# FFN1's half-word weight copies on GpSimd, and a new load and rank order, in a fused attention and two-FFN kernel

## The chip, the cores and the metric

One core of a Trainium2 chip runs the whole program. The metric is the device time of one execution in microseconds (us). The core has five engines with their own instruction streams, which run in order and meet through semaphores: TensorE (PE, products), VectorE (DVE), ScalarE (ACT), GpSimd (POOL) and SyncE (SP, which here issues nearly all DMAs).

## The reference, cut to what matters

Windowed attention (4 batches, 8 heads, 576 positions, window 64), then two feed-forward layers over 2304 tokens of width 512.

```python
def _attn_ref(q, k, v):                       # (4, 8, 576, 64) each
    scores = scale * np.matmul(q, k.transpose(0, 1, 3, 2))
    mask = (rel >= 0) & (rel < 64)
    scores = np.where(mask, scores, -1000000000.0)
    ...                                       # softmax
    return np.matmul(attn, v)

def _moe_ref(x, w_in, w_out):                 # FFN1: 512 -> 2048 -> 512
    h = np.maximum(x @ w_in, 0.0)
    return h * h @ w_out

def _moe2_ref(x, w_in, w_out, g_ln):          # FFN2: 512 -> 1024 -> 512
    h = x @ w_in
    ...                                       # softmax over h, h * softmax, layer norm with g_ln
    return ln @ w_out
```

The weights of both layers are 64-bit floats in memory. The kernel makes each into a 32-bit number by bit operations, and then into a pair (high part, rest), so that one product of 32-bit accuracy is three products on TensorE.

## The kernel before, in words

Sequence blocks of 64 positions are taken two at a time, a *unit*. Attention for the first four units (eight blocks) and FFN1 over their 512 tokens come first; units 4 and later are computed among FFN1's products and put aside in DRAM. The rest of FFN1 runs in two passes of 768 and 1024 tokens by a scheme with seven instead of eight block products, and then FFN2.

FFN1's 32 weight tiles are 16 of `w_in` (kind "a") and 16 of `w_out` (kind "b"), 128 x 512 each. A tile goes through `assembled` and `weights`:
- `load`: SyncE loads the raw 64-bit tile, 512 KB, into one of four `wraw` buffers;
- `top` (the *half-word copy*, a CAST at L260): every fourth 16-bit word of the raw tile is copied into the upper halves of a 32-bit tile `top`, of which there are two that take turns;
- `rest` (L265): VectorE shifts the raw tile's other words and ORs `top` in (SCALAR_TENSOR_TENSOR); this frees the raw buffer and the `top` tile;
- `first` (L283): ScalarE writes the high part, `wa` or `wb`; `second` (L286): VectorE writes the rest.

The products with `wa` are `ps_h` (L690), those with `wb` are `ps_y` (L706). Before them ScalarE and VectorE make the pair of x (`high`, `rest`, L530 and L533), and between them relu, square and the pair `g` (L636, L639). A unit of attention is scores (`ps_s`, L435), maximum, exponentials (L450), normalisation (`e<-e,sums`, L460), transposes (`ps_p`, L476 and L478), a copy, and values (`ps_v`, L516 to L521). For later units the normalisation is GpSimd's.

The order of all instructions comes from a planner, `Plan`: each step is added with its engine, an estimated length, a rank, what it follows and which buffers it takes and gives; `run` picks the step that can start first, the lower rank first, and `emit` writes the steps in that order. A step with `port=True` is not planned beside another such step. A table, `SHIFT`, adds a number to the ranks of single steps. Where TensorE would be idle in the plan, dummy products on a tile of ones (`ps_warm`, L1781) are put: 51 *fillers* in all, in the first part and late. `TOPS` is 16, the number of tiles of each kind, so VectorE makes all 32 half-word copies. The variable `by_dve` says so, and the copy is planned with the port.

Of the kernel before, what the change touches and what calls it, by code (L numbers as in the profile page):

```python
# [26 lines left out]
class Plan:  # L27
# [7 lines left out]

    HOP = {"DVE": 0.16, "ACT": 0.14, "POOL": 0.35, "PE": 0.12, "SP": 0.1}
    GAP = {"DVE": 0.1, "ACT": 0.1}
    SHIFT = {0: 13.59, 43: 8.08, 162: -11.77, 188: 6.06, 192: -3.28, 195: 10.82, 198: 10.82, 214: 13.42, 260: -3.43, 263: -3.43, 331: -39.05,
# [6 lines left out]

    def __init__(self, slots):
        self.tasks, self.slots = [], {k: [0.0] * n for k, n in slots.items()}
# [1 line left out]
    def add(self, eng, us, rank, fn, after=(), take=(), give=(), port=False, late=0.0, at=0.0):  # L49
        t = dict(eng=eng, us=us, rank=rank + self.SHIFT.get(len(self.tasks), 0.0), fn=fn, after=[a for a in after if a], take=take, give=give, port=port, late=late, at=at,  # L50
                 start=None, n=len(self.tasks))
        self.tasks.append(t)
        return t
# [51 lines left out]
def kernel(  # L105
# [48 lines left out]
    V, S, G, T = nc.vector, nc.scalar, nc.gpsimd, nc.tensor  # L154
# [47 lines left out]
    with ExitStack() as c1:  # L202
# [16 lines left out]
        add = plan.add  # L219
# [5 lines left out]
        def assembled(kind, i, rank, after=()):  # L225
            early = kind == "a" and i < EARLY
            ringed = kind in "ab"
            by_dve = ringed and i < TOPS
            o = {}

            def load():
                o["raw"] = raw_p.tile([P, 1024], I32, tag="wraw", name="wraw", bufs=RAWS)
                nc.sync.dma_start(out=o["raw"].bitcast(U16)[:, : 4 * DM - 1], in_=SRC[kind][i][:, 1:])

            def home():
                if kind == "a":
                    if i // 2 not in w1:
                        w1[i // 2] = w1_p.tile([P, 2, 512], F32, tag="w1", name="w1")
                    o["m"] = w1[i // 2][:, i % 2]
                elif kind == "2o":  # L240
                    w2o[i] = w1_p.tile([P, 2, 512], F32R, tag="w1", name="w2o")
                    o["m"] = at_p.tile([P, 512], F32, tag="qk"[i % 2], name="w2m", bufs=1)
                else:
                    o["m"] = raw_p.tile([P, 512], F32, tag="wm", name="wm", bufs=WMB)
                if not ringed:
                    G.memset(o["m"], 0.0)

            def top():
                if ringed:
                    home()  # L250
                    if not tops:
                        tops.append(x_p.tile([P, 2, 512], F32, tag="xc", name="top", bufs=1))
                        G.memset(tops[0], 0.0)
                    o["turn"] = turns.pop(0)
                    o["t"] = tops[0][:, o["turn"]]
                else:
                    o["t"] = o["m"]
                to, word = o["t"].bitcast(F16)[:, 1::2], o["raw"].bitcast(BF16)[:, 2::4]
                if by_dve:
                    V.tensor_copy(to, word)  # L260
                else:
                    S.activation(out=to, in_=word, func=AF.Copy)

            def rest():
                V.scalar_tensor_tensor(out=o["m"].bitcast(I32), in0=o["raw"][:, ::2], scalar=13, in1=o["t"].bitcast(I32),  # L265
                                       op0=ALU.logical_shift_right, op1=ALU.bitwise_or)
                if ringed:
                    turns.append(o["turn"])

            a = add("SP", 1.7, rank - (LEAD if early else 9), load, after, take=["raw"], late=LATE, at=0.7)  # L270
            own = {"a": [], "2o": ["qk"[i % 2] + "2"]}.get(kind, ["wm"])
            z = [] if ringed else [add("POOL", 0.6, rank - 3, home, [a], take=own, port=True)]
            b = add(*(("DVE", 0.36) if by_dve else ("ACT", 0.77)), rank, top, [a, *z], take=["top", *own] if ringed else [], port=by_dve)
            return o, add("DVE", 0.62, rank, rest, [b], port=True, give=["raw", "top"] if ringed else ["raw"])

        def weights(kind, i, rank, after=()):
            pool, store = {"a": (wa_p, wa), "b": (wb_p, wb)}[kind]
            o, c = assembled(kind, i, rank, after)
            made[kind, i] = c

            def first():
                o["d"] = pool.tile([P, 2, 512], F32R, tag="wb" if kind == "b" else "wa", name=f"w{kind}")
                S.activation(out=o["d"][:, 0, :], in_=o["m"], func=AF.Copy)  # L283

            def second():
                V.tensor_tensor(out=o["d"][:, 1, :], in0=o["m"], in1=o["d"][:, 0, :].bitcast(F32), op=ALU.subtract)  # L286
                store[i] = o["d"]

            b = add("ACT", 0.54, rank, first, [c], take=["wa"] * (kind == "a"))
            ready[kind, i] = add("DVE", 0.61, rank, second, [b], port=True, give=["wm"] * (kind == "b"))  # L290
# [3 lines left out]
        def kept_w2(kind, i, rank, after):  # L294
            o, c = assembled(kind, i, rank, after)

            def store():
                nc.sync.dma_start(out=w2_dram[i], in_=o["m"])

            made[kind, i] = add("SP", 0.8, rank, store, [c], late=2.2, give=["wm"])  # L300

        def last_w2(kind, i, rank, after):
            o, c = assembled(kind, i, rank, [*after, *read_w[i]])

            def high():
                S.activation(out=w2o[i][:, 0], in_=o["m"], func=AF.Copy, scale=gcol[:, i : i + 1])

            def low():
                V.scalar_tensor_tensor(out=w2o[i][:, 1], in0=o["m"], scalar=gcol[:, i : i + 1], in1=w2o[i][:, 0].bitcast(F32), op0=ALU.mult,
                                       op1=ALU.subtract)  # L310

            c = add("ACT", 0.54, rank, high, [c])
            ready[kind, i] = add("DVE", 0.61, rank, low, [c], port=True, give=["qk"[i % 2] + "2"])
# [1017 lines left out]
        LATE, LATE_X, LATE_P, TOPS = 2.8, 4.43, 4.63, KF  # L1331
# [4 lines left out]
        LOADS = (10.92, 14.03, 17.81, 25.72, 19.77, 31.14)  # L1336
        CHUNKS = (15.8, 24.78, 29.24)
        V0, LATER, OUT = 5.26, 51.93, 2.41
        LEAD = 22.21
        SOON, EARLIER, LATE_POOL = 11.15, 0, False  # L1340
        WOS, WOL, WSL, SQ, P2AT, P4AT, SOON2, SOON3, LEAD2 = 3, 8, 8, 5, 13, 17, 14, 6, 3
        PUT, PUT0, PUT1, AGO, LATEB, WOP = 16, 10, 3, 0, 145, 12
# [492 lines left out]
```

## Time and profile before

| | us |
|---|---|
| time, median of 3 runs | 628.54 (628.41, 628.54, 631.99) |
| profiled execution, its time | 629.19 |
| its span, first to last instruction | 627.4 |
| TensorE busy | 619.7 (99%) |
| weight loads of TensorE busy | 523.8 (83%) |
| VectorE busy | 485.1 (77%) |
| ScalarE busy | 433.4 (69%) |
| GpSimd busy | 44.1 (7%) |

How to read it: matmuls are pipelined and their ends are modelled, so TensorE's busy time is not work at its peak; the fillers count as busy too. A wait shows as idle time in front of an instruction, with what ended it. The granted clock was full in every slice of the page. Spans on GpSimd are rough.

### The profile page before, as it was taken

Reading aid. Unit: us, or ns where it says so; the run is one execution under the profiler, and the core shown is the slowest. Engines: PE = TensorE matmul, PEld = TensorE weight load, DVE = VectorE, ACT = ScalarE, POOL = GpSimd, SP = SyncE. Lnnn points to the kernel's source line nnn. Section 1 sums busy time; section 2 is a strip of 40 time slices with the busy share of each in tenths; the row PEclk is TensorE's granted clock in tenths of the full one; section 3 lists DMA queues with packets and bytes.
Section 4 is the critical chain, followed back from the end, with each engine's and each line's share of the span. In section 5 each row is a group of like instructions: output and inputs, shape, how many; then the busy total and the mean of one; then the engine's idle time right before and its main releaser. Section 6 shows DMA issues by size and latency. Waiting matters only on the chain.

```text
span 627.4 us, 11566 instructions
## 1 busy us (share of the span) xinstructions
PE 619.7 (99%) x4009; PEld 523.8 (83%) x4009; DVE 485.1 (77%) x1129; ACT 433.4 (69%) x985; POOL 44.1 (7%) x80
## 2 busy tenths in 40 slices
PE   8999999999999999999999999999999999999997
PEld 4798888889999989998888887878788888888886
DVE  5999898297876762397988999998998986687440
ACT  5788777577877675467677676873787875776551
POOL 1000000001212110000000000000001110110010
PEclk9999999999999999999999999999999999999999
DMA  8888988446899999877688556985255565532351
GB/s 278 275 293 297 309 291 282 128 176 230 278 296 329 291 327 286 296 260 217 211 285 266 196 162 230 311 253 170 100 169 177 176 218 169 200 135 88 115 184 50
DMA packets 85450, 141.26 MB, mean 225 GB/s; under 512 B 7824, under 2 KB 49552, under 8 KB 85392
## 3 DMA queue, kind: packets, MB, share of 16 engines
q1 hardware_dynamic: 84704, 140.14, 67.7%
q8 instruction: 31, 0.51, 0.3%
q10 hardware_dynamic: 688, 0.39, 0.2%
q14 instruction: 27, 0.22, 0.1%
HBM read 90.69 MB, written 49.81 MB: 224 GB/s over the span
## 4 chain that ended last, share of the span: by engine, by line
PE 90%; DMA 4%; DVE 3%; ACT 1%; issue 1%; SPq 1%; ACTq 0%; DVEq 0%
PE ps_h L935 21%; PE ps_o L1706 16%; PE ps_h L1545 14%; PE ps_y L1255 11%; PE ps_y L1069 8%; PE ps_y L706 7%; PE ps_h L690 6%; PE ps_s L435 3%; PE ps_v L518 2%; PE ps_v L521 1%; PE ps_warm L1781 1%; PE ps_p L478 1%; DMA kt<-in_k 1%; DMA qk<-in_k 1%; DMA r<-r_dram 1%
## 5 line engine op out<-in xcount | busy, mean ns | idle before, releaser
L1706 PE MATMUL ps_o<-w2o,lnT 128*128 128x512 f32 x432 | 99.2, 389 | 0.0
L1706 PEld LDWEIGHTS ps_o<-w2o,lnT 128*128 128x128 f32 x432 | 81.1, 188 | 16.9
L1255 PE MATMUL ps_y<-g,wb 128*128 128x384 f32 x384 | 71.9, 335 | 0.0
L1255 PEld LDWEIGHTS ps_y<-g,wb 128*128 128x128 f32 x384 | 66.8, 188 | 0.7 <-issue 0.3
L1545 PE MATMUL ps_h<-w2i,xx 128*128 128x512 f32 x243 | 62.6, 390 | 0.0
L1069 PE MATMUL ps_y<-g,wb 128*128 128x512 f32 x234 | 58.2, 390 | 0.1
L935 PE MATMUL ps_h<-xa,wo 128*128 128x512 f32 (+1 forms) x192 | 53.5, 370 | 0.1
L1545 PEld LDWEIGHTS ps_h<-w2i,xx 128*128 128x128 f32 x243 | 45.6, 188 | 9.6
L1069 PEld LDWEIGHTS ps_y<-g,wb 128*128 128x128 f32 x234 | 43.7, 188 | 10.1 <-DVE wb L1043 0.5
L935 PE MATMUL ps_h<-xb,wo 128*128 128x384 f32 (+1 forms) x192 | 51.0, 356 | 0.0
L706 PE MATMUL ps_y<-g,wb 128*128 128x512 f32 (+1 forms) x240 | 47.8, 352 | 0.0
L690 PE MATMUL ps_h<-x,wa 128*128 128x512 f32 (+1 forms) x240 | 47.4, 351 | 0.0
L935 PE MATMUL ps_h<-xo,wo 128*128 128x512 f32 (+1 forms) x128 | 47.2, 369 | 0.0
L450 ACT ACTIVATE e<-e,nmax 128x128 f32<-128x128 f32 x112 | 43.4, 390 | 2.6 <-DVE nmax L439 2.5
L690 PEld LDWEIGHTS ps_h<-x,wa 128*128 128x128 f32 x240 | 38.3, 189 | 6.6 <-issue 0.5
L706 PEld LDWEIGHTS ps_y<-g,wb 128*128 128x128 f32 x240 | 38.5, 189 | 6.0 <-issue 0.2
L935 PEld LDWEIGHTS ps_h<-xa,wo 128*128 128x128 f32 x192 | 35.2, 188 | 5.8 <-ACT u L959 0.8
L1695 ACT ACTIVATE lnT<-l 128x512 fp32r<-128x512 f32 x36 | 22.2, 627 | 24.3 <-PE ps_o L1706 22.0
L639 DVE TENSOR_TENSOR g<-r,g 128x384 fp32r<-128x384 f32 (+2 forms) x36 | 20.2, 566 | 22.6 <-ACT g L636 22.5
L935 PEld LDWEIGHTS ps_h<-xb,wo 128*128 128x128 f32 x192 | 34.4, 188 | 3.4 <-issue 0.3
L1545 PE MATMUL ps_h<-w2x,xx 128*128 128x512 f32 x135 | 36.8, 391 | 0.0
L1699 DVE TENSOR_TENSOR lnT<-l,lnT 128x512 fp32r<-128x512 f32 x36 | 24.1, 681 | 11.8 <-ACT lnT L1695 11.3
(182 smaller groups left out, 1257.9 us busy)
## 6 DMA issues: line engine op xcount, KB each, us to landing
wraw<-in_w_in SPq DMA_DIRECT2D x24, 511.8 KB, 5.6
wraw<-in_w_out SPq DMA_DIRECT2D x24, 511.8 KB, 5.4
vt<-in_v SPq DMA_DIRECT2D x32, 256.0 KB, 4.1
wo_dram<-wo SPq DMA_DIRECT2D x16, 512.0 KB, 5.1
wo<-wo_dram SPq DMA_DIRECT2D x16, 512.0 KB, 4.8
t_dram<-h SPq DMA_DIRECT2D x16, 512.0 KB, 3.0
l<-t_dram SPq DMA_DIRECT2D x64, 128.0 KB, 2.8
kt<-in_k SPq DMA_DIRECT2D x16, 384.0 KB, 5.5
```

Of the source, the lines that this page charges most:

```text
L435: T.matmul(to, qt[rows, i, hp, :], kt[rows, keys, hp, :], start=not begins, stop=not begins or hp == hps[-1])
L450: S.activation(out=o["er"][:, a, w], in_=s, func=AF.Exp, scale=SCALE if begins else -1.0, bias=o["nmax"][:, a, w : w + 1], accum_out=o["su ...
L639: V.tensor_tensor(out=o["g"][:, 1, :N], in0=o["r"], in1=o["g"][:, 0, :N].bitcast(F32), op=ALU.subtract)
L690: T.matmul(ps[:, :N], wa[kk][:, wi, c * P : c * P + P], xs[t][:, xi, c, n0:n1], start=n == 0, stop=n == 3 * DC - 1)
L706: T.matmul(acc[t, 0][d][:, n0:n1], wb[kk][:, wi, d * P : d * P + P], o["g"][:, xi, :N], start=kk == 0 and n == 0 and n0 == 0, stop=last an ...
L935: T.matmul(to[:, :N], w["t"][:, wi, off + c * P : off + c * P + P], (lo if xi else hi)()[:, c], start=begins and m == 0, stop=m == 5, skip ...
L1069: T.matmul(acc[name][d][:, :N], wb[kk][:, wi, col + d * P : col + d * P + P], q["g"][:, xi, :N], start=j == 0 and n == 0 and name not in ( ...
L1255: T.matmul(acc[t, half][d][:, :N], wb[kk][:, wi, d * P : d * P + P], q["g"][:, xi, :N], start=pos == 0 and n == 0, stop=pos == KF - 1 and ...
L1545: T.matmul(o[bank], o["xx", k][:, xi, at : at + P], w2i[w, r][wi][0](), start=begins and m == 0, stop=m == 5, skip_group_check=True)
L1695: S.activation(out=parts2(o["l", hf][:, 0]), in_=turned2(hf), func=AF.Copy)
L1699: V.tensor_tensor(out=parts2(l[:, 1]), in0=turned2(hf), in1=parts2(l[:, 0].bitcast(F32)), op=ALU.subtract)
L1706: T.matmul(o["o"], o["l", hf][:, xi, kk % 4, :], w2o[kk][:, wi, :], start=kk == 0 and n == 0, stop=kk == KF2 - 1 and n == 2)
```

## The change

Three things. Half-word copies of FFN1's weight tiles with an index of 2 or more (`POOLS = 2`; 14 of each kind, 28 of 32) are made by GpSimd (`G.tensor_copy`); the four with index 0 and 1 stay on VectorE. `SHIFT` holds other numbers, so the order on all engines is another. In SyncE's order the first unit's v goes behind the first q and k loads, and the second unit's v goes up in front of the weights.

```diff
-    SHIFT = {0: 13.59, 43: 8.08, 162: -11.77, 188: 6.06, 192: -3.28, 195: 10.82, 198: 10.82, 214: 13.42, 260: -3.43, 263: -3.43, 331: -39.05,
...
+    SHIFT = {0: -81.61, 6: 14.17, 10: -101.81, 19: -5.92, 20: -101.77, 37: 8.49, 55: -15.05, 160: -97.51, 161: -96.51, 162: -103.77, 177: 0.69,
...
-            by_dve = ringed and i < TOPS
+            by_dve, by_pool = ringed and i < TOPS, ringed and i >= POOLS
...
-                if by_dve:
+                if by_pool:
+                    G.tensor_copy(to, word)
+                elif by_dve:
                     V.tensor_copy(to, word)
...
-            b = add(*(("DVE", 0.36) if by_dve else ("ACT", 0.77)), rank, top, [a, *z], take=["top", *own] if ringed else [], port=by_dve)
+            b = add(*(("POOL", 0.6) if by_pool else ("DVE", 0.36) if by_dve else ("ACT", 0.77)), rank, top, [a, *z], take=["top", *own] if ringed else [], port=by_dve)
...
-        LEAD = 22.21
+        LEAD, POOLS = 22.21, 2
```

SyncE's first loads before (`vt` is v, `qt` and `kt` are q and k of a unit, `qk` those of the second unit, `wraw` a raw weight tile):

```order
L400 DMA vt_193<-in_v 64x512 x2
L383 DMA qt_198<-in_q 128x2x128 x2
L383 DMA qk_219<-in_q 128x2x256
L384 DMA qk_220<-in_k 128x2x256
L233 DMA wraw_237<-in_w_in 128x2047
L233 DMA wraw_255<-in_w_out 128x2047
L233 DMA wraw_294<-in_w_in 128x2047
L389 DMA qt_330<-in_q 128x512
L390 DMA kt_331<-in_k 128x768
L233 DMA wraw_371<-in_w_in 128x2047
L400 DMA vt_400<-in_v 64x512 x2
L233 DMA wraw_421<-in_w_out 128x2047
```

and now:

```order
L386 DMA qt_193<-in_q 128x2x128 x2
L386 DMA qk_206<-in_q 128x2x256
L387 DMA qk_207<-in_k 128x2x256
L403 DMA vt_230<-in_v 64x512 x2
L403 DMA vt_245<-in_v 64x512 x2
L234 DMA wraw_255<-in_w_in 128x2047
L234 DMA wraw_293<-in_w_in 128x2047
L392 DMA qt_323<-in_q 128x512
L393 DMA kt_324<-in_k 128x768
L234 DMA wraw_375<-in_w_in 128x2047
L234 DMA wraw_400<-in_w_out 128x2047
L234 DMA wraw_432<-in_w_out 128x2047
```

The first v moved from the front to behind q and k, the second from the eleventh place to the fifth, and the first `w_out` tile behind three of `w_in`.

VectorE around the third unit's maxima (TENSOR_REDUCE), before:

```order
L444 TENSOR_REDUCE nmax_416<-ps_s_413 128x4
L445 TENSOR_SCALAR nmax_416<-nmax_416 128x4
L444 TENSOR_REDUCE nmax_416<-ps_s_423 128x4
L445 TENSOR_SCALAR nmax_416<-nmax_416 128x4
L286 TENSOR_TENSOR wa_451<-w1_323,wa_451 128x512
L533 TENSOR_TENSOR x_373<-ps_v_454,x_373 128x2x128 x2
L260 CAST top_324<-wraw_371 128x512
L455 TENSOR_SCALAR sums_417<-sums_417 128x4
L456 RECIPROCAL sums_417<-sums_417 128x4
L265 SCALAR_TENSOR_TENSOR w1_489<-wraw_371,top_324 128x512
L460 TENSOR_TENSOR e_415<-e_415,sums_417 128x512
```

and now:

```order
L447 TENSOR_REDUCE nmax_416<-ps_s_413 128x4
L448 TENSOR_SCALAR nmax_416<-nmax_416 128x4
L447 TENSOR_REDUCE nmax_416<-ps_s_421 128x4
L448 TENSOR_SCALAR nmax_416<-nmax_416 128x4
L268 SCALAR_TENSOR_TENSOR w1_456<-wraw_375,top_346 128x512
L263 CAST top_346<-wraw_400 128x512
L458 TENSOR_SCALAR sums_417<-sums_417 128x4
L459 RECIPROCAL sums_417<-sums_417 128x4
L268 SCALAR_TENSOR_TENSOR wm_491<-wraw_400,top_346 128x512
L463 TENSOR_TENSOR e_415<-e_415,sums_417 128x512
L263 CAST top_346<-wraw_432 128x512
```

The x pair of the second unit (L533) now stands ahead of these rows, and the tile `wraw_375` has its shift-and-or without a cast: that cast is GpSimd's.

TensorE at the third unit's transposes (`ps_p`) and the first product with `wb` (`ps_y`), before:

```order
L478 MATMUL ps_p<-ident,e 128x128 x4
L435 MATMUL ps_s<-kt,qt 64x128 x16
L478 MATMUL ps_p<-ident,e 128x128 x4
L706 MATMUL ps_y<-g,wb 128x256 x12
L690 MATMUL ps_h<-x,wa 128x256 x24
L521 MATMUL ps_v<-pt,vt 64x64 x16
L478 MATMUL ps_p<-ident,e 128x128 x8
L706 MATMUL ps_y<-g,wb 128x256 x12
```

and now (a LDWEIGHTS and a MATMUL of `ones` are one filler):

```order
L481 MATMUL ps_p<-ident,e 128x128 x4
L1784 LDWEIGHTS ones
L1784 MATMUL ps_warm<-ones 128x512
L709 MATMUL ps_y<-g,wb 128x256 x12
L419 LDWEIGHTS ident_b
L419 MATMUL ps_s<-mask_b,ident_b 128x512
L438 MATMUL ps_s<-kt,qt 64x128 x16
L481 MATMUL ps_p<-ident,e 128x128 x4
L1784 LDWEIGHTS ones
L1784 MATMUL ps_warm<-ones 128x512
```

Fillers that stood ahead of the first FFN1 product (37 before, 26 now) stand behind it, among these rows; the first `ps_y` moved ahead of the fourth unit's scores.

## Rows read from the trace of the kernel before

**Rows 1.** Page, part 1: busy us (share of the span) xinstructions by engine

```profile
PE 619.7 (99%) x4009; PEld 523.8 (83%) x4009; DVE 485.1 (77%) x1129; ACT 433.4 (69%) x985; POOL 44.1 (7%) x80
```

**Rows 2.** Chain that ended last, 46 to 136 us: shares by engine and line

```profile
by line: PE ps_y L706 43.4%; PE ps_h L690 39.7%; PE ps_s L435 6.0%; PE ps_v L521 4.8%; PE ps_p L478 3.9%; PE ps_v L518 2.4%
```

**Rows 3.** Window: us, busy (xinstructions) of PE, PEld, DVE, ACT, POOL; PEclk, DMA, GB/s

```profile
20.00:100.00 80.00, 79.45 (x833) 67.66 (x824) 76.04 (x235) 65.49 (x216) 0.00 (x0) 1.00 0.90 303
```

**Rows 4.** Chain that ended last, start of the kernel: start us, us, what

```profile
0.72 0.60 SPq L400
...
1.37 0.58 SPq L400
...
3.65 5.46 DMA qk<-in_k
...
9.24 0.46 PE ps_s L435 x16
...
11.97 1.83 PE ps_warm L1781 x8
```

**Rows 5.** Timeline, TensorE: start us, us, instruction, shapes, count [idle before <-releaser]

```profile
21.76 1.72 PE L690 MATMUL ps_h<-x,wa 128*128 128x256 f32 x12
...
24.14 0.63 PE L478 MATMUL ps_p<-ident,e 128*128 128x128 f32 x4 [0.21 <-DVE sums L455]
...
45.92 0.29 PE L435 MATMUL ps_s<-kt,qt 64*64 64x128 f32 x1 [0.34 <-DMA kt<-in_k]
```

**Rows 6.** Timeline, TensorE, fillers and wait, late

```profile
388.62 1.04 PE L1781 MATMUL ps_warm<-ones 128*128 128x512 bf16 x4
...
417.18 5.54 PE L1069 MATMUL ps_y<-gx,wb 128*128 128x512 f32 x23 [0.23 <-DVE gx L1093]
...
447.04 2.12 PE L1781 MATMUL ps_warm<-ones 128*128 128x512 bf16 x9
```

**Rows 7.** Timeline, SyncE's DMA issues: first weight, second unit's v

```profile
4.16 0.47 SPq L233 DMA_DIRECT2D wraw<-in_w_in  x1
...
9.12 1.17 SPq L400 DMA_DIRECT2D vt<-in_v  x2
```

**Rows 8.** Timeline, VectorE: first cast, and sums of the second unit

```profile
11.36 0.46 DVE L260 CAST top<-wraw 128x512 f16<-128x512 bf16 x1
...
13.62 0.17 DVE L455 TENSOR_SCALAR sums<-sums 128x4 f32<-128x4 f32 x1 [0.70 <-ACT e L450]
```

**Rows 9.** Tile top, VectorE, 20 to 100 us: ns min/median/max, first to last start

```profile
L260 DVE CAST top<-wraw x26: 425/456/472, 22.1 to 95.9; 128x512 f16<-128x512 bf16 x26
```

**Rows 10.** Groups by line and form, GpSimd: xcount | busy us, mean ns | idle before

```profile
L460 POOL TENSOR_TENSOR e<-e,sums 128x512 f32<-128x512 f32 x16 | 17.5, 1116 | 208.0 <-DVE sums L456 196.1 <-ACT wo L884 11.9
...
L246 POOL MEMSET wm<- 128x512 f32 x8 | 4.2, 528 | 89.3 <-DVE g L639 35.7 <-DVE w2o L309 27.8 <-DMA r_dram<-u 12.9
```

**Rows 11.** Timeline, GpSimd, its first multiplications

```profile
147.12 2.04 POOL L460 TENSOR_TENSOR e<-e,sums 128x512 f32<-128x512 f32 x2 [143.87 <-DVE sums L456]
161.05 2.04 POOL L460 TENSOR_TENSOR e<-e,sums 128x512 f32<-128x512 f32 x2 [11.89 <-ACT wo L884]
...
176.01 2.36 POOL L460 TENSOR_TENSOR e<-e,sums 128x512 f32<-128x512 f32 x2 [8.42 <-DVE sums L456]
```

**Rows 12.** Timeline, VectorE in the same stretch

```profile
153.08 0.55 DVE L639 TENSOR_TENSOR g<-p,g 128x384 fp32r<-128x384 f32 x1
...
162.40 1.11 DVE L639 TENSOR_TENSOR g<-u,g 128x384 fp32r<-128x384 f32 x1
163.43 0.68 DVE L887 TENSOR_TENSOR wo<-w,wo 128x512 fp32r<-128x512 f32 x1
...
177.38 1.52 DVE L887 TENSOR_TENSOR wo<-w,wo 128x512 fp32r<-128x512 f32 x1
```

**Rows 13.** Chain that ended last, end of FFN1's first part

```profile
136.30 3.15 PE ps_h L935 x18
```

13 rows, old and new, of the table SHIFT are left out of this document.

## The prediction

> **What bounds the kernel now.** I read the page's first part first: TensorE is busy 99% of the span [rows 1]. That busy time is modelled, so I looked for its waits instead. The chain of work that ended last, asked for 46 to 136 us, holds TensorE alone: its shares by line are products, scores, transposes and values, and no other engine has a share [rows 2]. VectorE is almost as full there: over 20 to 100 us it is busy 76.04 of 80 us [rows 3], so 3.96 us idle. Two engines are full, but only TensorE sets the end; VectorE would take over if its work grew by more than about those 4 us.
>
> The chain leaves TensorE at the start and late. At the start [rows 4] it runs through SyncE, which issues the first unit's two v loads (from 0.72 us, 0.60 and 0.58 us, until 1.95 us), then q and k, then through the landing of the second unit's k (5.46 us, until 9.11 us), and then TensorE with the second unit's scores at 9.24 us. Between there and 22 us TensorE is filled with dummy products on `ones` (ps_warm): eight of them are one piece of 1.83 us, 0.23 us each. The first FFN1 product starts at 21.76 us and the third unit's transposes wait 0.21 us for VectorE at 24.14 us [rows 5]. After that only one wait is left in the first 136 us, 0.34 us for a k tile at 45.92 us. Late, TensorE has thirteen more fillers (four at 388.62 us, nine at 447.04 us) and a wait of 0.23 us at 417.18 us [rows 6]. So what can be had is: the way to the first scores, the fillers, and about a microsecond of scattered waits.
>
> **The change, part by part.**
>
> *Loads.* The first SyncE rows change most. Before, two v loads lead and take until 1.95 us; the second unit's k is issued at 3.65 us [rows 4]. After, q and k lead, and both units' v follow. The two issues in front cost 0.60 + 0.58 us and 0.05 us between and behind, 1.23 us from 0.72 to 1.95 us. That stretch lies on the chain, so q, k, the scores at 9.24 us and what hangs on them come 1.23 us earlier. If the landing of k (5.46 us) shortens because 256 KB of v no longer go ahead of it, there is a little more; if it is bound by bytes in flight, there is less. I take 1.2 us. The first weight, issued at 4.16 us before, had one pair of v loads ahead of it and now has two; the second pair took 1.17 us to issue [rows 7], so it goes out at about 5.3 us. Its half-word copy starts at 11.36 us before [rows 8] and in the new order stands behind the second unit's sums, at 13.62 us before [rows 8] and 1.2 us earlier now, so about 12.4 us. Even a landing 1.1 us later is covered; were it not, the loss would be that 1.1 us. The second unit's v, issued at 9.12 us before [rows 7], is issued near 4.1 us. Its values products now stand earlier on TensorE, and the first FFN1 product has 26 fillers in front of it instead of 37. Eleven fillers at 0.23 us would be 2.5 us, but they are not gone: up to about 45 us the order has 39 fillers after against 38 before, and in the late stretch 12 against 13 [rows 6]. So the work is only put earlier among the fillers, and the sum of fillers (51) is unchanged: +0.2 us early, -0.2 us late, zero together.
>
> *Copies.* 28 casts leave VectorE, 456 ns each, 12.8 us. Of these I look at the stretch 20 to 100 us, where 26 casts lie [rows 9]; four of all stay on VectorE, two of them early, so about 24 go, 10.9 us. On GpSimd no row has this copy. It is bounded below by the memset of the same 512 words, which only writes, 528 ns, and above by the product of two tensors, 1116 ns [rows 10]. A copy reads one tensor, so it lies between; I take 0.8 us. 28 times 0.8 us is 22 us, 31 us at the upper end. GpSimd's first operation after the masks is the one at 147.12 us, after 143.87 us idle [rows 11]. The change adds one wait per weight: VectorE's shift-and-or now waits for GpSimd. Behind the first of these, in VectorE's new order, stand a cast, the third unit's sums and its normalisation, for which TensorE's transposes wait (0.21 us at 24.14 us before). A weight is copied some 3 us apart (26 in 74 us), and four raw tiles cover the added 0.3 to 0.7 us. If that cover fails, in-order SyncE waits at the next weight, behind it q, k and v of a later unit, as at 45.92 us, 0.34 us there before [rows 5].
>
> *The port.* GpSimd and VectorE disturb one another. While GpSimd multiplies from 161.05 us (two operations, 2.04 us), VectorE's subtraction for g takes 1.11 us where it takes 0.55 us alone; during the pair from 176.01 us (2.36 us) a weight subtraction takes 1.52 us against 0.68 us [rows 11, 12]. So a cast can give back its gain. Bounds: nothing (VectorE is in an operation from PSUM, or waits), or the whole of the cast. I take half of 0.8 us, 0.4 us, which leaves VectorE about where it was (24 times 0.056 us, 1.3 us less). As TensorE did not wait for VectorE there, that pays nothing either way. The Trainium skill, SBUF — State Buffer, section "SBUF: two separate sides", speaks against this change: it states that the port pair is an exclusive lock, so that of a GpSimd operation and a VectorE operation with two SBUF inputs, the one that starts later waits for the whole of the other. The stretched rows agree with it. By that rule a cast that always meets such an operation costs VectorE its whole length, and the time is that of the slower rival below. The Trainium skill, GPSIMD Engine Reference, section "3.1 Elementwise", gives about 1.03 cycles an element for a body with one input; an estimate from that page is 0.44 us and a start-up for 512 elements, by which the sum would stay as it is.
>
> *New ranks.* They reorder TensorE's pieces from 136 us on without adding any. The waits and fillers there [rows 6] can move by some tenths; I take zero, with 1 us either way.
>
> **Sum.** The profiled execution took 629.19 us, 627.4 us of them span. Less 1.2 us for the loads, fillers +0.2 and -0.2, copies and ranks 0: 628.0 us. This execution lies 0.65 us above the median of the three runs, 628.54 us; the same step from the median gives 627.3 us.
>
> **The rivals.**
>
> *No gain.* The scores of the first unit also need k, issued on ScalarE's queue, which the change leaves as it is, and if the first 10 us are bound by the DMA engines, q and k land when they did. For it: the long landing of 5.46 us. Against it: fewer bytes go ahead. Or fillers and ScalarE's exponentials, which did not change, take up the 1.2 us. Time: 628.5 us.
>
> *Slower: the port makes VectorE the bound.* Place: 20 to 100 us. VectorE loses 0.456 us of work per cast and gains what it is blocked. With 24 casts and 3.96 us idle it decides at 0.456 + 3.96/24 = 0.62 us blocked per cast. If every cast of 0.8 us blocks wholly, VectorE's work grows 24 times 0.8 less 0.456, 8.3 us, 4.3 us more than its idle time: 627.3 + 4.3 = 631.6 us. At 1.12 us each it is 16.0 us, 12 us too much: 639 us. For it: the head of the kernel is full of two-input operations (shift-and-or, subtractions). Against it: beside GpSimd operations of about 1 us each the rows show 0.56 and 0.84 us blocked, and for another operation of the second line nothing (0.68 us at 163.43 us) [rows 12]; VectorE's reductions and masked scores read PSUM.
>
> *More gain.* VectorE's relief is used: the 0.34 us wait at 45.92 us, the 0.21 us at 24.14 us and the 0.23 us at 417.18 us go, and some of the late 3 us of fillers hide waits that the new ranks shorten. All of it together, 0.8 + 1.2 + up to 2 us: 624.5 us. Against it: the fillers stay in the order.
>
> **How the numbers follow.** Forecast 0.50; no gain 0.21; slower by the port 0.19, of which 0.09 beyond 1%; more gain 0.10, of which 0.04 beyond 1% (a measurement of this kernel can tell about 1%, 6.3 us, from no change). So faster by over 1% 0.04, within 1% 0.87, slower by over 1% 0.09. The range runs from the larger gain to the blocked port with casts of 0.8 us and the disorder of the ranks: 624.8 to 632.6 us.
>
> **What would show it.** Right: the second unit's scores near 8.0 us instead of 9.24 us; the first FFN1 product near 19 to 20 us; the second transposes near 22.9 us; 28 casts on GpSimd of 0.5 to 1.1 us, VectorE's casts down to 4, some of its two-input operations between 20 and 100 us well over 0.68 us; TensorE without waits from 30 to 136 us. Wrong: casts over 1 us on GpSimd, a wait of TensorE for VectorE before 100 us, or the end of FFN1's second products, 136.30 us before [rows 13], later than 136 us; that place should come at about 135 us. If it comes at 135 us and the end does not move, the new ranks after it have lost the gain.

## The result and the profile after

The changed kernel is slower. Its median is 632.81 us (12 runs, 631.37 to 635.44), that of the kernel before in the same session 629.30 us (12 runs, 628.41 to 632.52). The ratio is 1.0054 with a 95% interval of 1.0036 to 1.0071: 2.3 to 4.5 us more, and less than 1%. (The ratios, here and below, are taken over all runs of a session and can differ from the quotient of the two medians by up to 0.1%.) The forecast, 627.3 us, had the wrong sign, and 632.81 us lies just above its range.

The profiled execution of the changed kernel took 631.37 us, with a span of 629.5 us. It is the shortest of its twelve runs, 1.4 us under their median, so its trace shows the loss smaller than it usually is. Part 1 of the page (columns as in [rows 1]):

```profile
PE 621.1 (99%) x4009; PEld 523.6 (83%) x4009; DVE 480.1 (76%) x1101; ACT 436.0 (69%) x985; POOL 70.3 (11%) x108
```

Against [rows 1], 28 instructions have left VectorE (DVE) and stand on GpSimd (POOL). The same stretch as in [rows 3], 20 to 100 us, by windows:

```profile
20.00:100.00 80.00, 79.74 (x805) 66.80 (x805) 72.09 (x209) 65.45 (x214) 23.02 (x24) 1.00 0.89 298
```

VectorE's busy time fell from 76.04 to 72.09 us. TensorE's granted clock is 1.00 in both. So the two things that the change does by name were done. TensorE's timeline at the start of the changed kernel (start us, us, engine line, operation, out<-in), lines three higher than before:

```profile
7.99 0.46 PE L438 MATMUL ps_s<-qk 64*64 64x64 f32 x16
...
18.92 1.77 PE L693 MATMUL ps_h<-x,wa 128*128 128x256 f32 x12
20.53 0.82 PE L1784 MATMUL ps_warm<-ones 128*128 128x512 bf16 x3
```

The second unit's scores start at 7.99 us (9.24 us in [rows 4]), the first FFN1 product at 18.92 us (21.76 us in [rows 5]). But the chain of work that ended last, at the end of FFN1's first part, answers to [rows 13] with no lead left, 136.36 us against 136.30 us:

```profile
136.36 3.15 PE ps_h L938 x18
```

Where the time is lost shows much later. This is the chain of the changed kernel between 340 and 372 us (start us, us, what; SPq is SyncE's queue). In the kernel before, the chain of the same stretch is TensorE alone. First its shares by line, then the changed kernel's chain:

```profile
by line: PE ps_h L935 72.4%; PE ps_y L1069 28.3%
```

```profile
346.41 0.70 DVE u L624
...
349.48 0.69 DVE tt L1122
350.17 0.61 DVE wb L1046
...
350.79 0.33 SPq L234
...
351.18 5.01 DMA tt_dram<-tt
...
356.21 0.69 DVE wf L1033
...
362.42 0.61 DVE u L624
...
363.07 4.38 PE ps_h L938 x18
```

It reads: VectorE finishes `tt`, one of the sums that stand in the four raw buffers. SyncE has a weight load (L234) in front of the store of `tt`. That load waits for a raw buffer until VectorE's subtraction `wb` is done, so the store goes out at 351.18 us and lands 5.01 us later. Only then does VectorE start `wf` (L1033, the first sum of the transform that `replaced` makes out of two weights), because `wf` was given the buffer in which `tt` stood. Everything behind `wf` in VectorE's order is late, up to the eviction `u` (L624), which TensorE's next product needs. VectorE's and TensorE's waits for this, each from the list of waits (total us, times, longest):

```profile
DVE wf L1033 <- DMA tt_dram<-tt: 0.6, 1, 0.6
...
PE ps_h L938 <- DVE u L624: 0.4, 1, 0.4
PE ps_y L1072 <- DVE wb L1046: 0.7, 1, 0.7
PE ps_h L1548 <- ACT u L1562: 0.4, 1, 0.4
```

In this short run the place costs little. The other two waits end at 409.84 and 468.45 us.

### The profile page after: what moved, and what is told of

Read it like the earlier page. It is cut to its first block, busy times and chain, and to the rows that moved or that the text cites. A ratio compares the mean times of both kernels' runs of the same rounds, so it can differ in the third digit from the quotient of the medians.

```text
span 629.5 us, 11625 instructions
## 1 busy us (share of the span) xinstructions
PE 621.1 (99%) x4009; PEld 523.6 (83%) x4009; DVE 480.1 (76%) x1101; ACT 436.0 (69%) x985; POOL 70.3 (11%) x108
## 4 chain that ended last, share of the span: by engine, by line
PE 92%; DVE 3%; DMA 2%; ACT 1%; issue 1%; SPq 0%; POOL 0%; ACTq 0%; POOLq 0%; DVEq 0%
PE ps_h L938 20%; PE ps_o L1709 16%; PE ps_h L1548 14%; PE ps_y L1258 11%; PE ps_y L1072 9%; PE ps_h L693 7%; PE ps_y L709 7%; PE ps_s L438 3%; PE ps_v L521 2%; PE ps_warm L1784 2%; PE ps_v L524 1%; PE ps_p L481 1%; DMA r<-tt_dram 1%; DMA tt_dram<-tt 1%; DMA r_dram<-u 1%
## 5 line engine op out<-in xcount | busy, mean ns | idle before, releaser
L261 POOL CAST top<-wraw 128x512 f16<-128x512 bf16 x28 | 27.0, 967 | 78.5 <-DMA wraw<-in_w_in 29.6
```

Source lines behind the costliest of these rows:

```text
L261: G.tensor_copy(to, word)
```

## The experiments

Most of the kernels below hold both tables of ranks. The planner runs once with each, which gives two orders of the same tasks: `A`, the changed kernel's, and `B`, that of the kernel before. Each kernel then says which is used, and up to where; the place where one order takes over from the other is the *seam*. The time of the kernel before was taken again beside each group of kernels and is given with the first of them, or with each. `R` names the theory that the new order of the work behind FFN1's first part costs the time, `P` the rival that the copies on GpSimd and the port that they share with VectorE do.

**One part at a time: the order alone, the copies alone.** In the first kernel the order is the changed kernel's and all copies are VectorE's; in the second the order is that of before and 28 copies are GpSimd's.

```diff
-                if by_pool:
-                    G.tensor_copy(to, word)
-                elif by_dve:
+                if by_dve:
...
+        plan.order = A
```

> The changed kernel's order on every engine, but all 32 half-word copies made by VectorE, each in the place where GpSimd's stood. Theory R (the new ranks after FFN1's first part cost the time): still 3 to 4 us slower than before, about 632.8 us, or a little more since VectorE has 12.8 us of casts again. Theory P (GpSimd's copies, 0.97 us each, block VectorE through the shared port and cost the time): back to 629.3 us or below.

Measured: 633.66 us against 629.72 us, ratio 1.0062 (1.0049 to 1.0076).

```diff
+        plan.order = B
```

> The kernel before, in its order, but 28 of the copies on GpSimd. Theory R: as before, 629.3 us within 1 us, since TensorE did not wait for VectorE there. Theory P: 2 to 4 us slower, 631.5 to 633 us, the loss between 20 and 136 us in the trace.

Measured: 629.50 us, ratio 0.9995 (0.9984 to 1.0007). The whole loss is there without one copy on GpSimd, and it is gone with all 28 of them. `P` falls. That the copies gain nothing either is seen too.

**The order, in two halves.** The seam is the end of FFN1's first part, at about 136 us.

```diff
+        cut = {t["n"] for t in B[:530]}
+        plan.order = [t for t in A if t["n"] in cut] + [t for t in B if t["n"] not in cut]
```

> The changed kernel's order with copies on GpSimd up to the end of FFN1's first part, the order of before behind it. Theory R: as before, 629.3 us within 1 us (the first part ended at 136.36 us against 136.30 us in the two traces). Theory P: as the changed kernel, 632.8 us.

Measured: 629.27 us, ratio 0.9998 (0.9988 to 1.0008).

The other way round, with the copies on VectorE:

```diff
+        cut = {t["n"] for t in A[:531]}
+        plan.order = [t for t in B if t["n"] in cut] + [t for t in A if t["n"] not in cut]
```

> The order of before with copies on VectorE up to the end of FFN1's first part, the changed kernel's order behind it. Theory R: as the changed kernel, 632.8 us. Theory P: as before, 629.3 us.

Measured: 632.69 us, ratio 1.0040 (1.0024 to 1.0056). So the new loads, the new head and the copies together neither gain nor lose, and the loss belongs to the order behind 136 us.

**Later seams.** `A` up to a task near 293 us, and up to one near 400 us, then `B`.

```diff
+        cut = {t["n"] for t in B[:1231]}
+        plan.order = [t for t in A if t["n"] in cut] + [t for t in B if t["n"] not in cut]
```

> The changed kernel's order and GpSimd copies as far as about 293 us, the order of before behind that. Theory R-late (what costs the time stands behind 300 us, where the changed kernel's chain goes over VectorE from 346.4 to 363.1 us and TensorE has pauses at 362.3, 398.5, 408.8, 432.8 and 467.7 us): 629.0 to 630.0, as before. Rival R-spread (the new ranks lose a little everywhere): about half of the 3.5 us, 631. Rival: the head's lead of 2.5 us at the first FFN1 product is kept where the rest is old: 627.

Measured: 632.10 us against 629.11 us, ratio 1.0041 (1.0025 to 1.0056). No expectation holds, and the time says nothing for or against them. Right at the seam, from 300.70 to 303.88 us, the chain leaves TensorE for ScalarE and VectorE, and TensorE waits there twice, 0.7 and 0.9 us, as in no other kernel, so the seam itself makes a loss. Ahead of it, from 136 to 300 us, TensorE has no wait in this execution.

```profile
300.72 0.60 ACT u L979
...
303.22 0.61 DVE c L641
```

The second differs from it by the number alone, `B[:1683]`.

> The changed kernel's order as far as about 400 us, the order of before behind that. If the place near 350 to 365 us (a transform's first step on VectorE stands behind the store of tt, which holds the raw buffer) is the main part of the loss: plus 0.7 to 2.5 us over before, 630.0 to 631.8. If the loss is behind 400 us (408.8, 432.8, 467.7 us): as before, 629 to 630. The seam itself may cost something; then it is above 632.

Measured: 632.22 us, ratio 1.0048 (1.0029 to 1.0067), above the first range of the expectation. TensorE has one wait near this seam, 0.4 us at 401.75 us for a `gx` of VectorE. Behind it the order is the old one, so most of the 3.1 us is lost before 400 us, and the place that the changed kernel's chain pointed at is larger here. The chain of that kernel, with the landing that it goes through, and then VectorE's wait and TensorE's wait between 340 and 372 us:

```profile
352.53 6.35 DMA tt_dram<-tt
...
358.90 0.69 DVE wf L1050
```

```profile
DVE wf L1050 <- DMA tt_dram<-tt: 1.9, 1, 1.9
...
PE ps_h L955 <- DVE u L641: 1.4, 1, 1.4
```

In the first kernel of this section the same landing took 6.84 us and VectorE waited 2.4 us, in the fourth (old head, new rest) it was 6.35 and 1.9 us; TensorE waited 1.4 us in both, as here. In the execution of the changed kernel shown above it was 5.01, 0.6 and 0.4 us.

**Is it this wait?** This cause can be taken away without moving one instruction. The four raw buffers are taken in turn as the allocator finds them free. The next three kernels write that turn down as a string of buffer numbers, and from `wf` on they exchange two numbers: `wf` gets the buffer that VectorE itself had emptied just before, and the following `tt` gets the one whose store is still under way. On every engine the instructions stand exactly as before the exchange.

```diff
-    raw_p = ctx.enter_context(tc.tile_pool(name="raw", bufs=2))
+    raw_pool = ctx.enter_context(tc.tile_pool(name="raw", bufs=2))
...
+            return raw_pool.tile(shape, dtype, tag="wraw" + next(at_slot), name=name, bufs=1)
```

> The changed kernel, every instruction in its place, but from one allocation on two of the four raw buffers are exchanged: the transform's sum (wf, whose turn on VectorE came at 356.2 us only when the store of tt had landed) takes a buffer that VectorE itself has freed, and the next tt takes that of the stored tt. Theory W (this wait is the main part of the loss): VectorE's wait there (0.57, 1.9 and 2.4 us in three runs with landings of 5.0, 6.35 and 6.84 us) and TensorE's behind it (0.5 to 1.6 us) are gone, 631.0 to 631.8 against 632.8. Rival: something else is late at the same point (TensorE waits as long there, for another row): 632.8.

Measured: 631.22 us against 629.17 us, ratio 1.0025 (1.0014 to 1.0035); the changed kernel had 632.81 us and 1.0054. VectorE starts `wf` at 356.87 us without a wait, and in the chain TensorE runs through. (This start is later than the 356.21 us above because this execution comes late to the whole stretch; it lost 1.0 us at 191 us, see below.)

```profile
350.43 4.08 PE ps_h L964 x18
...
359.95 1.36 PE ps_y L1098 x6
361.31 6.81 PE ps_h L964 x30
```

The same exchange in the kernel with `A` up to 400 us:

> The changed kernel's order to about 400 us, the order of before behind, with the same exchange of two raw buffers. Without the exchange it took 632.2 and TensorE waited 1.6 us at 364 us. Theory W: 630.0 to 630.6, of which 0.5 to 1 us over before stand in the third unit's stage (165 to 245 us). Rival: 632.

Measured: 630.24 us, ratio 1.0015 (1.0006 to 1.0023); without the exchange it was 632.22 us and 1.0048. The members of a pair were timed in different sessions, so each is set against the kernel before of its own session: by the medians the one wait costs 1.5 us in the first pair and 2.0 us in the second, by the ratios 1.8 and 2.1 us, with about 1.3 us of noise either way on each. By the medians that is two fifths of the loss in the first pair and two thirds in the second. No kernel was run in which the turn is written down and nothing exchanged, so that the writing down itself helps is not ruled out by a run of its own; what speaks against it is that the kernel before, with its turn written down in the same way, is no faster (next).

The reverse in the kernel before: its `wf` at 356.66 us is given the buffer of the stored `tt`.

> The kernel before, every instruction in its place, but the transform's sum that starts at 356.66 us takes the raw buffer of the stored tt, as in the changed kernel. tt is ready at 352.1 us; its store is issued at 352.12 and lands after 5.0 to 6.8 us, so at 357.1 to 359.0: VectorE would wait 0.5 to 2.3 us. Theory W: 0.3 to 1.6 us slower than before, 629.4 to 630.7. Rival (before has slack on VectorE here): VectorE waits, TensorE does not, 629.1.

Measured: 629.52 us, ratio 1.0003 (0.9994 to 1.0012). VectorE does wait, and TensorE has no wait in that stretch:

```profile
DVE wf L1057 <- DMA tt_dram<-tt: 0.3, 1, 0.3
```

```profile
DMA to landing us min/median/max: 4.9/5.1/5.1
```

The second row is the time to landing of that kernel's three `tt` stores between 335 and 372 us. 629.52 us lies at the lower end of theory W's range, but the interval holds "no change" as well, and the trace reads as the rival says: VectorE waits, TensorE does not. The wait itself is small because `tt` is stored as soon as it is ready and lands in 5.1 us. So in the old order this buffer does no harm that can be measured: the landing is short there, and TensorE has some slack. Which of the two spares it was not tried.

**The late part alone.** `B` up to about 390 us, `A` behind that, copies on VectorE.

```diff
+        cut = {t["n"] for t in A[:1600]}
+        plan.order = [t for t in B if t["n"] in cut] + [t for t in A if t["n"] not in cut]
```

> The kernel before until about 390 us, the changed kernel's order behind that (VectorE makes the copies). In the changed kernel TensorE has waits at 408.8 (0.84 us, for wb on VectorE) and 467.7 us (0.56 us, for u on ScalarE) that before lacks. If they are a part of the loss: 0.6 to 1.4 us over before, 629.8 to 630.6. If they only follow from a later start of that stretch: as before, 629.1.

Measured: 629.95 us, ratio 1.0013 (1.0004 to 1.0022), 0.8 us over before. The chain goes over VectorE and ScalarE at the same two places, though the part ahead of them is the old one:

```profile
406.37 1.88 DVE w2i L363 x3
408.25 0.58 DVE g L1111
...
409.38 0.69 DVE wb L1061
...
410.12 1.93 PE ps_y L1087 x7
...
467.55 0.62 ACT xx L1538
468.18 0.49 ACT u L1577
...
468.71 1.43 PE ps_h L1563 x5
```

On VectorE three weight products (`w2i`) and a `g` stand ahead of `wb`, which TensorE's `ps_y` needs, and on ScalarE an `xx` stands ahead of `u`, which the next `ps_h` needs. That is not what is new: in the kernel before both engines have these instructions in the same order. Its VectorE, its ScalarE and its TensorE:

```profile
406.48 0.68 DVE L1093 TENSOR_TENSOR g<-r,g 128x512 fp32r<-128x512 f32 x1
407.08 1.28 DVE L1043 TENSOR_TENSOR wb<-wf,wb 128x512 fp32r<-128x512 f32 x2
```

```profile
466.08 0.62 ACT L1520 ACTIVATE xx<-xr 128x512 fp32r<-128x512 f32 x1
466.61 0.59 ACT L1559 ACTIVATE u<-ps_h 128x512 f32<-128x512 f32 x1
```

```profile
465.33 8.32 PE L1706 MATMUL ps_o<-w2o,lnT 128*128 128x512 f32 x36
```

At the second place TensorE's own order is what changed. Before, 36 products `ps_o` cover the time in which ScalarE makes `u`; in the new order six more `ps_h` stand ahead of the `ps_o` and wait for it, 0.4 us in this kernel's list as in the changed kernel's. At the first place the changed kernel waits 0.7 us because its `wb` comes 1.4 us later than before; its chain there goes through a load from `tt_dram` and the `gx` made from it:

```profile
399.02 5.09 DMA r<-tt_dram
...
404.21 0.64 ACT gx L1093
```

In this section's kernel that wait is too short to be listed. What the rest of the 0.8 us is was not tried.

**What is left.** The table has TensorE's waits of 0.3 us and more behind 136 us, in the six executions whose order from 136 to 400 us is the new one (us; a dash is no such wait, "old" the old order at that place; waits at and behind the seam at 400 us are left out). The kernel before has none of them; its longest wait there is 0.2 us.

| execution | time | k tile, 191 us | `u`, 318 us | `u` behind `wf` | `wb`, 410 us | `u`, 470 us |
|---|---|---|---|---|---|---|
| changed kernel | 631.37 | - | - | 0.4 | 0.7 | 0.4 |
| its order, copies on VectorE | 635.06 | 1.7 | - | 1.4 | - | 0.4 |
| old head, new rest | 633.45 | 0.4 | 1.6 | 1.4 | - | 0.4 |
| `A` to 400 us | 632.39 | 0.8 | - | 1.4 | old | old |
| changed kernel, buffers exchanged | 631.45 | 1.0 | - | - | - | 0.4 |
| `A` to 400 us, buffers exchanged | 631.37 | 1.3 | 0.3 | - | old | old |

So a second wait is about as large as that for `wf`, and it too hangs on a landing: TensorE waits for a k tile at 191 us in five of these six, but not in the short execution of the changed kernel, nor in that of the kernel with `A` to 293 us. The chain of the exchanged changed kernel there:

```profile
184.16 0.38 SPq L418
...
184.59 6.68 DMA kt<-in_k
...
191.40 1.10 PE ps_s L464 x32
```

No kernel was run that takes this wait away. The wait at 318 us is large in one execution alone, 1.6 us behind a weight load that took 8.52 us to land.

**Where the head's lead went.** Two kernels leave out dummy products (their results are not used). The first has the new head and the old rest, without the 12 that stand behind the first FFN1 product; the second is the kernel before without its 13 late ones.

```diff
+        first = next(k for k, t in enumerate(plan.order) if t["fn"].__name__ == "product")
+        plan.order = [t for k, t in enumerate(plan.order) if k < first or k > 600 or t["rank0"] != 900.0]
```

> The new head with the old rest, without the 12 dummy products (their results are not used) that stand behind the first FFN1 product; 39 of 51 are left. In the trace of the changed kernel the head's lead of 2.5 us at the first FFN1 product (19.22 against 21.76 us) is gone at 40 us, and the dummy products between 19 and 40 us are 12 x 0.216 = 2.6 us long. Theory F (the dummy products themselves give the lead back): about 2.5 us less than with them, 626.7. Rival C (they only stand in pauses for weights that come at the rate of the loads): no change, 629.3. Rival K (without them the granted clock falls for a while): slower than 630.

Measured: 629.16 us against 629.11 us, ratio 1.0002 (0.9991 to 1.0014). (The timeline's row for the first product reads 18.92 us, not the 19.22 us of that text.) Twelve fillers are 12 x 0.23 = 2.8 us of TensorE, and without them nothing changes that can be measured. The chain from 12 to 44 us is then VectorE's, with a k tile at its end, for which TensorE waits 1.1 us:

```profile
35.31 0.33 SPq L251
35.73 0.38 SPq L409
36.16 7.58 DMA kt<-in_k
43.87 1.10 PE ps_s L455 x32
```

```diff
+        plan.order = [t for k, t in enumerate(plan.order) if k < 600 or t["rank0"] != 900.0]
```

> The kernel before without its 13 late dummy products (388.62 and 447.04 us; results not used); 38 are left. If they hold TensorE longer than the pauses they stand in: down by up to 13 x 0.216 = 2.8 us, 626.5. If they stand in pauses that are there anyway: 629.3, no change. If the granted clock falls in those pauses without them: slower than 630.

Measured: 629.73 us against 629.11 us, ratio 1.0002 (0.9991 to 1.0012). Here, too, the dummies stood in pauses that are there anyway: TensorE now waits 1.1 us for ScalarE at 449.22 us, where nine of them stood. The granted clock stays full (1.00) in both kernels.

None of these kernels is faster than the kernel before by more than its interval.

## Why the prediction was wrong, step by step

**Loads, -1.2 us.** Right where it was worked out, wrong in what was made of it. The second unit's scores came 1.25 us earlier, as forecast (8.0 us). The first product came 2.84 us earlier, with 11 fillers fewer ahead of it. But the sum carried this 1.2 us to the end of the kernel, and at 136 us it was all gone: 136.36 us, where I had 135 us and called anything later than 136 us a sign of being wrong. The rival "No gain" had this outcome, but not its cause: q and k did land earlier, and fillers left out gave nothing back (its third cause, ScalarE's exponentials, was not tried). The kernel without the 12 fillers points at a better one: from 12 to 35 us its chain is VectorE's, and a k load that stands in SyncE's queue behind a weight load comes when VectorE has freed a raw buffer. In that trace an earlier start moves the wait, not the end. That the same holds in the changed kernel, whose chain is TensorE with its fillers there, is argued and not shown.

**Fillers, zero.** Right. Neither the 12 nor the 13 hold TensorE in a way that the time shows.

**Copies, zero; 0.8 us each, half of it blocked.** The total was right (second kernel: 0.9995). The size was low. The group of all 28 casts (busy us, mean ns, then idle time of GpSimd ahead of them and its releasers), and the second kernel's window of 20 to 100 us (us, VectorE busy, granted clock, DMA share, GB/s):

```profile
L261 POOL CAST top<-wraw 128x512 f16<-128x512 bf16 x28 | 27.0, 967 | 78.5 <-DMA wraw<-in_w_in 29.6 <-DMA wraw<-in_w_out 18.1 <-DVE e L463 9.5
```

```profile
20.00:100.00 80.00, 74.70 (x209) 1.00 0.89 300
```

A cast takes 967 ns on average, inside the bounds of 528 and 1116 ns but nearer the upper one (the longest took 1273 ns). The 0.44 us that the prediction estimated beside its sum is less than half of it; the measurement decides. A block per cast was taken as 0.4 us, with VectorE 1.3 us less busy. In the old order with GpSimd's copies VectorE was busy 74.70 us between 20 and 100 us, 1.34 us less than the 76.04 us of [rows 3]: some 24 casts of 0.456 us are 10.9 us, so 9.6 us came back, about 0.4 us a cast, as taken. The cast's length and the half were guesses, so that they meet is luck. In the new order it is 3.95 us less, 0.29 us a cast.

**The port.** Real, and no bound. One pair in the changed kernel, GpSimd and then VectorE:

```profile
60.62 0.98 POOL L261 CAST top<-wraw 128x512 f16<-128x512 bf16 x1 [3.36 <-DMA wraw<-in_w_out]
```

```profile
60.89 1.21 DVE L289 TENSOR_TENSOR wa<-w,wa 128x512 fp32r<-128x512 f32 x1
62.02 0.68 DVE L289 TENSOR_TENSOR wb<-wm,wb 128x512 fp32r<-128x512 f32 x1
```

A subtraction of two SBUF tiles that meets a cast takes 1.21 us, the next one alone 0.68 us. The Trainium skill, SBUF — State Buffer, section "SBUF: two separate sides", says that such an operation waits for the whole of a GpSimd operation that began first; this trace agrees with it in the direction: the subtraction began 0.27 us after the cast, 0.71 us of the cast were left, and it lost 0.53 us. The slower rival asked for 0.62 us a cast before VectorE becomes the bound; 0.29 to 0.40 us were measured, and between 20 and 100 us the changed kernel's TensorE has no wait for VectorE (in the second kernel it has one of 0.4 us, at 32.70 us, and the end is as before). One of the arguments against that rival was a misreading: the 0.68 us operation at 163.43 us [rows 12] was beside no GpSimd operation, since the pair from 161.05 us had ended at 163.09 us [rows 11].

**New ranks, "I take zero, with 1 us either way".** This is the step that failed. The prediction read how the table reorders the first 46 us and gave everything behind 136 us two sentences: no piece is added, so no time. The runs show about 3 us there, 3.0 us for the old head with the new rest and 3.5 us for the whole order. What it left out is what a piece waits for when it moves. One wait of VectorE for a landing store, through the buffer that a tile is given, is 1.5 to 2 us of it; that was shown by taking it away, in two kernels. The late part is 0.8 us (`B` up to 390 us) to 1.0 us (the two exchanged kernels, 631.22 less 630.24). What is left of the exchanged kernel with `A` up to 400 us over before, 1.07 us (0.4 to 1.4 us by its interval), stands between 136 us and its seam. In that stretch its TensorE waits 1.3 us for a k tile at 191 us, which the kernel before doesn't do; that this wait is the cause is argued from the traces and was not tried. The prediction had written a test, "If it comes at 135 us and the end does not move, the new ranks after it have lost the gain". It did not come at 135 us: the gain was lost before, and the ranks lost more.

**Chances and range.** Within 1% had 0.87, and 0.5% it is; most of that chance stood on causes that did not act. The range ended at 632.6 us by the blocked port and 1 us of disorder. That the measured 632.81 us lies so near is luck, since the port was no bound; the true term had 1 us of width where it needed 4. Of the 5.5 us between forecast and measurement, 3.5 us are the ranks, 1.2 us the loads' gain that did not last, and 0.8 us the kernel before itself, whose median is 629.30 us in twelve runs where the three at hand had 628.54 us.

## What to carry to other kernels

When a change hands a planner new ranks, its stated edits may be the small part: read the order on every engine to the end, and ask of each buffer of a shared ring who had it last. Here a buffer whose last user was a store was free only when the store had landed, 5 to 7 us after its issue. Given to `wf`, with evictions queued behind it on VectorE, it cost TensorE up to 1.4 us; given to the next `tt`, which comes later, it cost nothing. And a lead at the start of the kernel is to be checked at the first place where the chain is one engine alone, not at its source: here 1.2 us at 9 us were nothing at 136 us.

## What the runs showed of the hardware

Stores of the same 512 KB take different times in the two orders and from run to run. The times to landing of the three `tt` stores between 335 and 372 us, in the changed kernel and in the kernel before:

```profile
DMA to landing us min/median/max: 5.0/6.0/7.1
```

```profile
DMA to landing us min/median/max: 5.0/5.1/5.6
```

All DMA engines together moved 233 GB/s in the changed kernel between 340 and 372 us and 212 GB/s in the kernel before. The one store that `wf` waits for took 5.01, 6.35, 6.35 and 6.84 us in four runs of this order, and VectorE's wait behind it 0.57, 1.9, 1.9 and 2.4 us; the first of these is the 631.37 us execution, the last one took 635.06 us. Why it lands later was not tried.
